# Attention, routing and experts on one core: values in 32-column tiles, sums beside the next pair's values, one-hot matrices in blocks of eight columns

## The chip, the core and the metric

The kernel runs on one core of a Trainium2 chip as one launch. The metric is the device time in microseconds (us). Five engines work side by side and wait for each other through semaphores: PE (TensorE: matmuls; its weight loads are listed apart as PEld), DVE (VectorE), ACT (ScalarE), POOL (GpSimd) and SP, which here only issues transfers.

## The reference, cut to what matters

```python
# 1. attention over 4 batches x 12 heads, 448 rows, head size 64
q_n, k_n = rmsnorm(q, g_q), rmsnorm(k, g_k)
scores = q_n @ k_n.T / 8
attn = softmax(scores)                 # row sums divide the product below
x = (attn @ v)                         # -> [1792 tokens, 768]
# 2. routing: 8 experts, each takes at most 224 of the 1792 tokens
logits = x @ w_gate                    # [1792, 8]
order = argsort(-logits.flatten())     # greedy: best (token, expert) first
# a token goes to the first expert in that order that still has room
# 3. each expert: relu(x[mask] @ w1[e]) @ w2[e]
# 4. h = x @ w_in;  out = (h * cos(h)) @ w_out
```

## The kernel before, in words

The program is written down by a small planner (class `Plan`): every instruction becomes a step with a cost from a table (`Plan.cost`), the data it reads and writes, and a latest time; `Plan.run` then fixes one order for each engine. The order on the chip is that list, and the chip's waits come from the data. The planner knows that PE pays for a change of tile shape (`P.switch`, 0.09 in the attention stage) and prefers the shape it is in (`SAME`).

**Attention** works through 24 pairs of heads. Keys stand on partitions in four chunks of 112. For a pair, `scores` writes exp(scores) of chunk c and head h to a tile `pf` (112 keys x 448 queries); GpSimd adds two chunks to a tile `pa` (ring of `NPA` = 6) for the row sums. `weigh` (L585) then multiplies values by these: for each chunk and head one fp32 matmul with a stationary 112x64 block of `vr` and the 448 columns of `pf` moving, into the 64 partitions of the head in the accumulator `po`. So the array is used as two tiles of 64 columns, one for each head. Two chunks form one `block`, which the planner keeps together; a pair has two of them. ScalarE copies `po` to `xe`. Then come `sums` (L603; row sums with a stationary of ones) and `logits` (L614; gate products of `xe`), fp32 matmuls with 112 moving columns in four tiles of 32 columns, into `dn`. The other matmuls of the stage are `st` (scores) and `s` (a bound of the row maximum; DVE reduces it to `cm`), whose stationary has 64 partitions, so that two of them use the halves of the array by rows, and transposes `t` and the histogram `dn<-ab`, which use the whole array; the transpose of `cm` has 7 columns. `finish(P_ - 1)` (L726) divides by the sums, adds up logits, and transposes `xe` for the token rows. While this goes on, DVE and ACT split weights of the later stages into two fp32r parts (`na`, `nr`) wherever there is room.

**Routing** finds for each expert in turn (t = 0 to 7) the tokens it takes. For t = 0 and 1 it is `quick` (L1005): a threshold is found in three digits of the logits. `count` (L952) builds for each of 16 columns of tokens two one-hot or step matrices `A` and `B` (`AB`; 112x128 bf16, one instruction each, on DVE, ten of the `B` on ACT), and PE multiplies them to a histogram; `digits` (L972) reads off the digit; `narrow` (L985) narrows the search. For t = 0 the first histogram has been built during attention (`start`, L993, one batch at a time), so two counts are left, and for t = 1 three. Then `phase` (L1074) ranks the tokens, builds 16 one-hot matrices `oh` (112x112), and PE turns them into the row numbers `idx`. GpSimd gathers those token rows (`xr<-x,idx`), PE transposes them (`tr`), and expert t starts. For t from 2 on the threshold is found by `slow`, beside the matmuls of earlier experts; only the `oh` part is the same.

**Experts and output.** PE works through two experts, then the cosine part for their 448 tokens, four times. `WARM_B` = 24 matmuls on `oh` keep PE at work while the first gather is under way. `RUSH`, `EARLIER` and `P.rush` are the planner's numbers for how early a routing shall come.

## Time and profile before

| what | us |
|---|---|
| median of 3 runs | 1138.01 (1130.66 to 1146.6) |
| the profiled execution, its own time | 1132.48 |
| its span, first to last instruction | 1130.7 |
| PE busy | 1080.5 (96%) |
| DVE busy | 888.5 (79%) |
| ACT busy | 638.2 (56%) |
| POOL busy | 251.8 (22%) |
| TensorE clock, mean granted share | 0.978 |

An fp32 matmul shows in the trace as two records, so a count of records of `po` or `dn` is twice that of the program's matmuls. A record's end is modelled and overlaps the next one's start; what a run of matmuls costs is read from the start of its first record to the start of the next run. Attention lasts to about 327 us, the first routing to about 364 us, and after that PE works on experts and output to the end.

### The profile page before, as it was taken

Reading aid. Unit: us, or ns where it says so; the run is one execution under the profiler, and the core shown is the slowest. Engines: PE = TensorE matmul, PEld = TensorE weight load, DVE = VectorE, ACT = ScalarE, POOL = GpSimd, SP = SyncE. Lnnn points to the kernel's source line nnn. Section 1 sums busy time; section 2 is a strip of 40 time slices with the busy share of each in tenths; the row PEclk is TensorE's granted clock in tenths of the full one; section 3 lists DMA queues with packets and bytes.
Section 4 is the critical chain, followed back from the end, with each engine's and each line's share of the span. In section 5 each row is a group of like instructions: output and inputs, shape, how many; then the busy total and the mean of one; then the engine's idle time right before and its main releaser. Section 6 shows DMA issues by size and latency. Waiting matters only on the chain.

```text
span 1130.7 us, 20923 instructions
## 1 busy us (share of the span) xinstructions
PE 1080.5 (96%) x7268; PEld 877.6 (78%) x7268; DVE 888.5 (79%) x2453; ACT 638.2 (56%) x1562; POOL 251.8 (22%) x367
## 2 busy tenths in 40 slices
PE   7999999999976999999999999999999999999997
PEld 5555555555535998997989998899989789999887
DVE  8888989999989968998988886568889577756300
ACT  5687878865663437664656672236666236646300
POOL 3677787766510000000110000020000002000001
PEclk9899999999985999999999999999999999999999
DMA  6353455455553798779877668748866958666652
GB/s 163 92 163 110 145 186 170 163 163 177 211 213 97 215 252 297 255 229 383 276 221 205 227 218 251 271 132 238 233 206 218 333 200 243 188 223 208 239 186 94
DMA packets 172745, 234.35 MB, mean 207 GB/s; under 512 B 14112, under 2 KB 144608, under 8 KB 168032
## 3 DMA queue, kind: packets, MB, share of 16 engines
q1 hardware_dynamic: 170240, 222.01, 61.8%
q0 software_dynamic: 2400, 11.01, 2.8%
q8 instruction: 57, 0.93, 0.3%
q14 instruction: 48, 0.39, 0.1%
HBM read 196.37 MB, written 36.52 MB: 206 GB/s over the span
## 4 chain that ended last, share of the span: by engine, by line
PE 41%; issue 14%; DVE 9%; DMA 6%; ACT 1%; POOL 1%; POOLq 0%; SPq 0%; DVEq 0%; ACTq 0%
PE acc L47 39%; DMA xr<-x,idx 2%; DMA ws<-in_moe_w_out_dram 2%; DMA ws<-in_moe_w_dram 2%; DVE oh L47 1%; DVE na L47 1%; DVE wx L47 1%; DVE AB L47 1%; PE rt L47 1%; DVE r L47 1%; PE tr L47 1%; DMA wx<-w_out 0%; ACT wx L1279 0%; POOL xr L1230 0%; DVE gl L47 0%
## 5 line engine op out<-in xcount | busy, mean ns | idle before, releaser
L47 PE MATMUL acc<-wx,gh 128*128 128x512 f32 (+1 forms) x896 | 226.7, 340 | 0.0
L47 PE MATMUL acc<-x2h,wx 128*128 128x448 f32 x768 | 223.0, 368 | 0.0
L47 PEld LDWEIGHTS acc<-wx,gh 128*128 128x128 f32 x896 | 155.7, 190 | 20.7 <-issue 3.0
L47 PEld LDWEIGHTS acc<-x2h,wx 128*128 128x128 f32 x768 | 144.5, 188 | 11.2
L47 PE MATMUL acc<-wx,gl 128*128 128x512 f32 (+1 forms) x448 | 150.6, 336 | 0.0
L47 PE MATMUL acc<-x2l,wx 128*128 128x448 f32 x384 | 140.2, 365 | 0.0
L47 PE MATMUL acc<-gh,wx 128*128 128x448 f32 (+1 forms) x768 | 129.7, 325 | 2.9 <-DVE gh L47 2.7
L47 POOL TENSOR_TENSOR pa<-pf,pf 112x448 f32<-112x448 f32 x94 | 111.8, 1209 | 71.3 <-ACT pf L47 71.2
L47 DVE TENSOR_TENSOR wx<-ws,wx 128x1024 fp32r<-128x1024 f32 (+1 forms) x96 | 104.5, 1089 | 27.2 <-ACT wx L1279 26.4
L47 PEld LDWEIGHTS acc<-gh,wx 128*128 128x128 f32 x768 | 116.4, 191 | 10.8 <-DVE gh L47 2.6
L1230 POOL DMA_INDIRECT xr<-x,idx x16 | 19.4, 1211 | 445.2 <-issue 141.3
L47 ACT ACTIVATE pf<-st 112x448 f32<-112x448 f32 x192 | 93.9, 540 | 42.5 <-PE st L47 40.9
L47 DVE TENSOR_REDUCE cm<-s 128x1 f32<-128x448 f32 x168 | 100.3, 619 | 17.6 <-PE s L47 15.6
L1279 ACT ACTIVATE wx<-ws 128x1024 fp32r<-128x1024 f32 (+1 forms) x96 | 90.7, 947 | 32.1 <-DMA ws<-in_moe_w_dram 16.5
L47 ACT ACTIVATE r<-r 128x448 f32<-128x448 f32 x128 | 74.0, 578 | 53.8 <-DVE r L47 52.0
L47 DVE SCALAR_TENSOR_TENSOR r<-r,acc 128x448 f32<-128x448 int32 (+1 forms) x128 | 77.8, 618 | 32.9 <-ACT r L47 31.4
L47 PE MATMUL acc<-xe,wx 128*128 128x448 f32 x576 | 91.9, 320 | 0.0
L47 PEld LDWEIGHTS acc<-wx,gl 128*128 128x128 f32 x448 | 85.1, 190 | 8.3
L47 PEld LDWEIGHTS acc<-xe,wx 128*128 128x128 f32 x576 | 86.2, 189 | 4.0
L47 PE MATMUL st<-qq,kk 64*112 64x448 f32 x576 | 88.5, 392 | 0.6 <-ACT pf L47 0.5
L47 ACT ACTIVATE oh<-oh 128x896 bf16<-128x896 bf16 x48 | 45.6, 949 | 75.2 <-DVE oh L47 74.9
L1432 POOL DMA_INDIRECT out_dram<-xo,to x14 | 15.6, 1113 | 319.3 <-ACT xo L1400 318.8
(269 smaller groups left out, 1990.3 us busy)
## 6 DMA issues: line engine op xcount, KB each, us to landing
wx<-w_in SPq DMA_DIRECT2D x64, 768.0 KB
wx<-w_out SPq DMA_DIRECT2D x36, 1024.0 KB
ws<-in_moe_w_dram SPq DMA_DIRECT2D x64, 384.0 KB
ws<-in_moe_w_dram SPq DMA_DIRECT2D x48, 512.0 KB
nr<-in_moe_w_in_dram SPq DMA_DIRECT2D x32, 384.0 KB
w_in<-nr SPq DMA_DIRECT2D x32, 384.0 KB
ws<-in_moe_w_out_dram SPq DMA_DIRECT2D x14, 512.0 KB
w_out<-wx SPq DMA_DIRECT2D x14, 512.0 KB
```

The lines of the kernel that those rows point to most:

```text
L47: self.plan.add([(self.eng, self.plan.cost(self.eng, name, out, r, kw), lambda: f(*args, **kw), self.plan.shares(self.eng, name, out, r, k ...
L1230: P.add([("POOL", 2.1 - 0.9 * h, lambda x=x, h=h: nc.gpsimd.indirect_dma_start(out=x, out_offset=None, in_=x_rows, in_offset=bass.Indirect ...
L1279: P.add([("ACT", 0.093 + n * 0.1067, lambda: nc.scalar.activation(hi, s, AF.Copy)), ("DVE", 0.07 + n * 0.0667, lambda: nc.vector.tensor_co ...
L1432: step = nc.gpsimd.indirect_dma_start(out=out, in_=src, in_offset=None, out_offset=bass.IndirectOffsetOnAxis(ap=at, axis=0)).ins
```

## The change

Values: the four 32-column blocks of the two heads' values each get a column tile of their own, so a block has 8 matmuls (two chunks, four tiles) where it had 4. The sums and gate products of pair P - 1 (`count`) are written inside the first values block of pair P, and `finish` follows one pair later; pairs 22 and 23, and the last sums, are taken up separately at the end. `NPA` goes from 6 to 8. In routing, `match` builds eight columns of `A`, `B` or `oh` with one bf16 `tensor_tensor` each, comparing a row of numbers with the columns' values, which are kept twice, side by side; ACT builds none of them any more, except in `start`, which keeps the old form as `signs`. `B` now holds 0 and 1 where it held -1/2 and 1/2, so `digits` halves the total and adds the rank itself. The planner's numbers move too: the price of the new matmuls, `P.switch` 0.09 to 0.18, `WARM_B` 24 to 28, `RUSH` for t = 3.

```diff
--- before.py
+++ after.py
             if name == "matmul" and rhs.dtype == F32 and self.beside:
-                if out.partition_size() == 32:
-                    return 0.05
-                passes *= {32: 0.32, 64: 0.893}.get(out.partition_size(), 1)
+                return 0.05 if out.free_size() <= CP else 0.61
...
-NPA = 6
+NPA = 8
...
         def weigh(P_):
 
-            po, pd = bo()[:, :S], bd()[:, 0:CP]
+            po = bo()[:, :S]
             t = vals.pop(P_).rearrange("p h (c d) -> p h c d", d=D)
             P.beside = True
             for c0 in range(0, NC, 2):
                 def both():
                     for c in range(c0, c0 + 2):
-                        for h in range(2):
-                            pe.matmul(po[h * D:(h + 1) * D], t[:, h, c], exps[P_, h, c], start=c == 0,
+                        for o in range(0, 2 * D, 32):
+                            h, d = divmod(o, D)
+                            pe.matmul(po[o:o + 32], t[:, h, c, d:d + 32], exps[P_, h, c], start=c == 0,
                                       stop=c == NC - 1)
+                    if c0 == 0 and P_ - 1 in open_:
+                        count(P_ - 1)
                 block(both)
-            sums_of[P_] = pd
+                if c0 == 0 and P_ == NPR - 2:
+                    P.beside = False
+                    finish(P_ - 1)
+                    P.beside = True
             outs[P_] = xes()
             sc.activation(outs[P_], po, AF.Copy)
-
-            def sums():
-                for h in range(2):
-                    halves = [c for c in (0, 2) if (P_, h, -1 - c) in exps]
-                    for c in range(0, NC, 2) if len(halves) == 2 else (0, 2, 3):
-                        n, e = CP + (c == 0), exps.pop((P_, h, -1 - c if c in halves else c))
-                        for j in range(NC):
-                            pe.matmul(pd[32 * j:32 * j + 32], ones[0:n, h], e[0:n, j * CP:(j + 1) * CP],
-                                      start=h == 0 and c == 0, stop=False)
-
-            block(sums)
-
-            def logits():
-                for j in range(NC):
-                    pe.matmul(pd[32 * j:32 * j + 32], wg[:, P_ % NP], outs[P_][:, j * CP:(j + 1) * CP], start=False,
-                              stop=True)
-
-            block(logits)
+            open_.add(P_)
+            if P_ >= NPR - 2:
+                block(lambda: count(P_))
             P.beside = False
+        open_ = set()
+        def count(P_):
+            open_.discard(P_)
+            pd = sums_of[P_] = bd()[:, 0:CP]
+            for h in range(2):
+                halves = [c for c in (0, 2) if (P_, h, -1 - c) in exps]
+                for c in range(0, NC, 2) if len(halves) == 2 else (0, 2, 3):
+                    n, e = CP + (c == 0), exps.pop((P_, h, -1 - c if c in halves else c))
+                    for j in range(NC):
+                        pe.matmul(pd[32 * j:32 * j + 32], ones[0:n, h], e[0:n, j * CP:(j + 1) * CP],
+                                  start=h == 0 and c == 0, stop=False)
+            for j in range(NC):
+                pe.matmul(pd[32 * j:32 * j + 32], wg[:, P_ % NP], outs[P_][:, j * CP:(j + 1) * CP], start=False,
+                          stop=True)
...
-            finish(P_ - 1)
+            finish(P_ - 2 + (P_ == NPR - 1))
...
-        P.switch = 0.09
+        P.switch = 0.18
...
+    def twice(self, x):
+        return x.unsqueeze(2).to_broadcast([*x.shape, 2])
+    def match(self, out, row, cols, op):
+        c, n = out.shape[1:]
+        sh = [out.shape[0], c, n // 2, 2]
+        self.nc.vector.tensor_tensor(out.rearrange("p c (n k) -> p c n k", k=2),
+                                     row.rearrange("p (n k) -> p n k", k=2).unsqueeze(1).to_broadcast(sh),
+                                     cols.unsqueeze(2).to_broadcast(sh), op=op)
...
+    def count(self, p, X, W, ab, n, whole=False):
+        nc, P = self.nc, self.P
+        for a in range(0, NCOL, 8):
+            cs = slice(a, a + 8)
+            self.match(ab[:, 0, cs], P["ia"][0:CP], X[:, cs], ALU.is_equal)
+            self.match(ab[:, 1, cs, 0:n], P["ib"][0:CP, 128 - n:], W[:, cs], ALU.is_le)
+            if whole:
+                nc.begin()
+            for c in range(a, a + 8):
+                nc.tensor.matmul(p[:, 0:n], ab[:, 0, c], ab[:, 1, c, 0:n], start=(c == 0), stop=(c == NCOL - 1))
+            if whole:
+                nc.finish()
+    def digits(self, p, n, T, signs=False):
         nc, P, v = self.nc, self.P, self.nc.vector
-        v.tensor_copy(P["tot"], p[:, 0:1].to_broadcast([128, 2]))
+        rp = P["rp2" if signs else "rpt"]
+        if signs:
+            v.tensor_copy(P["tot"], p[:, 0:1].to_broadcast([128, 2]))
+        else:
+            v.tensor_scalar(P["tot"], p[:, 0:1].to_broadcast([128, 2]), 0.5, None, op0=ALU.mult)
+            v.tensor_tensor(rp, P["tot"][:, 0:1].bitcast(F32), P["rp"], op=ALU.add)
         pa = self.psum()
         nc.tensor.matmul(pa[:, 0:2], P["up"], P["tot"], start=True, stop=True)
-        v.scalar_tensor_tensor(P["cmp"][:, 0:n], p[:, 0:n], pa[:, 0:1], P["rp2"].to_broadcast([128, n]), op0=ALU.add,
+        v.scalar_tensor_tensor(P["cmp"][:, 0:n], p[:, 0:n], pa[:, 0:1], rp.to_broadcast([128, n]), op0=ALU.add,
                                op1=ALU.is_ge, accum_out=P["acc"])
...
-        v.scalar_tensor_tensor(P["X"], F, T, X, op0=ALU.subtract, op1=ALU.add)
-        v.scalar_tensor_tensor(P["W"], F, T, W, op0=ALU.is_equal, op1=ALU.mult)
-        v.tensor_tensor(P["X"], P["X"], P["Z"], op=ALU.min)
+        v.scalar_tensor_tensor(P["XF"], F, T, X, op0=ALU.subtract, op1=ALU.add)
+        v.tensor_tensor(P["X"], self.twice(P["XF"]), self.twice(P["Z"]), op=ALU.min)
+        v.scalar_tensor_tensor(P["W"], self.twice(F), T, self.twice(W), op0=ALU.is_equal, op1=ALU.mult)
...
-        v.scalar_tensor_tensor(rel, half, float(-CP), rel, op0=ALU.mult, op1=ALU.add)
+        v.scalar_tensor_tensor(P["rel2"], self.twice(half), float(-CP), self.twice(rel), op0=ALU.mult, op1=ALU.add)
         v.tensor_tensor(pv[:, :, 1], P["pc"], half.unsqueeze(2).to_broadcast([CP, NCOL, 3]), op=ALU.mult)
...
-        for c in range(NCOL):
-            nc.either("tensor_scalar", oh[:, c], P["io"], rel[:, c:c + 1], None, op0=ALU.is_equal)
+        for a in range(0, NCOL, 8):
+            self.match(oh[:, a:a + 8], P["io"], P["rel2"][:, a:a + 8], ALU.is_equal)
         if not first:
...
-RUSH = (15.0, 4.0, 5.0)
+RUSH = (15.0, 4.0, 5.0, 12.0, 5.0, 5.0, 5.0, 5.0)
-WARM_B = 24
+WARM_B = 28
```

**PE, attention, about the tenth pair.** `po` values, `dn<-pa` row sums, `dn<-xe` gate products, `st` scores, `s` bounds; a buffer's number follows the name. Before:

```order
L47 MATMUL st_231<-sr_158,heads 112x448
L47 MATMUL s_229<-kk_147,qq_152 128x448
L47 MATMUL dn_233<-pa_210,ones 32x112 x4
L47 MATMUL dn_233<-pa_206,ones 32x112 x4
L47 MATMUL dn_233<-pa_211,ones 32x112 x4
L47 MATMUL dn_233<-pa_207,ones 32x112 x4
L47 MATMUL dn_233<-xe_216,wg 32x112 x4
L47 MATMUL s_229<-kk_148,qq_153 128x448
```

Now:

```order
L47 MATMUL s_232<-kk_150,qq_155 128x448
L47 MATMUL po_236<-pf_206,vr_170 32x448 x2
L47 MATMUL po_236<-pf_207,vr_170 32x448 x2
L47 MATMUL po_236<-pf_190,vr_170 32x448 x2
L47 MATMUL po_236<-pf_191,vr_170 32x448 x2
L47 MATMUL dn_237<-pa_208,ones 32x112 x4
L47 MATMUL dn_237<-pa_210,ones 32x112 x4
L47 MATMUL dn_237<-pa_209,ones 32x112 x4
L47 MATMUL dn_237<-pa_211,ones 32x112 x4
L47 MATMUL dn_237<-xe_220,wg 32x112 x4
L47 MATMUL st_234<-qq_153,kk_148 112x448
```

Sums and gate products stood between matmuls of other shapes; now they follow values of the same shape, and the values' matmuls are twice as many and half as wide.

**DVE, routing for t = 0, the first count.** `T` is the digit found last, `W` and `X` the columns' values, `ib` and `ia` the rows they are compared with. Before:

```order
L47 SCALAR_TENSOR_TENSOR W<-F_113,T_135,W_120 112x16
L47 SCALAR_TENSOR_TENSOR X<-F_113,T_135,X_117 112x16
L47 TENSOR_SCALAR AB<-ib,W 112x128
L47 TENSOR_TENSOR X<-X,Z 112x16
L47 TENSOR_SCALAR AB<-ib,W 112x128
L47 TENSOR_SCALAR AB<-ia,X 112x128 x6
```

Now:

```order
L47 SCALAR_TENSOR_TENSOR XF<-F_113,T_137,X_117 112x16
L47 SCALAR_TENSOR_TENSOR W<-F_113,T_137,W_120 112x32
L47 TENSOR_TENSOR X<-XF,Z 112x32
L47 TENSOR_TENSOR AB<-ib,W 112x1024
L47 TENSOR_TENSOR AB<-ia,X 112x1024 x2
L47 TENSOR_TENSOR AB<-ib,W 112x1024
```

The shown start of 22 short instructions becomes four long ones; PE's first product of the count needs the first two of them.

**PE, start of the first expert.** `tr` and `acc<-ident,xr` transposes of the gathered rows, `rt<-AB` products of the count for t = 1, `acc<-xo,ws` the expert's matmuls. Before:

```order
L47 MATMUL rt_4230<-tot,up 128x2
L47 MATMUL tr_4228<-ident,xr_4243 128x112 x2
L47 MATMUL tr_4229<-ident,xr_4243 128x112 x2
L47 MATMUL acc_4225<-ident,xr_4243 128x112 x2
L47 LDWEIGHTS ones
L47 MATMUL rt_4231<-acc_133,ones 128x8
L47 MATMUL tr_4228<-ident,xr_4244 128x112 x2
L47 MATMUL tr_4229<-ident,xr_4244 128x112 x2
L47 MATMUL acc_4225<-ident,xr_4244 128x112 x2
L47 MATMUL acc_4226<-xo,ws_4232 128x224 x6
L47 MATMUL acc_4227<-xo,ws_4233 128x224 x2
L47 LDWEIGHTS AB
```

Now:

```order
L47 MATMUL tr_4426<-ident,xr_4441 128x112 x2
L47 MATMUL tr_4427<-ident,xr_4441 128x112 x2
L47 MATMUL acc_4423<-ident,xr_4441 128x112 x2
L47 LDWEIGHTS AB
L47 MATMUL rt_4428<-AB 128x128
...
L47 MATMUL tr_4426<-ident,xr_4442 128x112 x2
L47 MATMUL tr_4427<-ident,xr_4442 128x112 x2
L47 MATMUL acc_4423<-ident,xr_4442 128x112 x2
...
L47 MATMUL acc_4424<-xo,ws_4430 128x224
L47 MATMUL rt_4429<-tot,up 128x2
```

The sixteen products of the second count for t = 1 came behind the expert's first eight matmuls; now eight of them stand between the transposes of the two halves of rows and eight ahead of the expert's first matmul.

## Rows read from the trace of the kernel before

**Rows 1.** The page's head.

```profile
span 1130.7 us, 20923 instructions
```

**Rows 2.** Stretches: length, busy us (instructions) by engine, granted clock, DMA share, GB/s.

```profile
85.00:250.00 165.00, 164.07 (x1538) 95.96 (x1536) 153.19 (x377) 128.35 (x427) 123.36 (x166) 1.00 0.48 154
250.00:330.00 80.00, 73.29 (x680) 41.09 (x676) 74.57 (x183) 50.02 (x114) 41.11 (x39) 0.98 0.56 196
330.00:365.00 35.00, 20.11 (x115) 15.15 (x116) 32.02 (x212) 12.04 (x39) 2.51 (x4) 0.55 0.44 139
365.00:400.00 35.00, 32.59 (x211) 30.12 (x211) 32.74 (x136) 17.61 (x43) 2.72 (x2) 0.97 0.74 220
400.00:1130.70 730.70, 714.58 (x4151) 648.71 (x4149) 525.65 (x1354) 371.66 (x718) 31.66 (x40) 1.00 0.72 231
```

**Rows 3.** PE's timeline, two places in attention: start, length, what, records.

```profile
185.22 1.73 PE L47 MATMUL po<-pf,vr 112*64 112x448 f32 x8
186.88 0.85 PE L47 MATMUL st<-qq,kk 64*112 64x448 f32 x6
187.56 0.36 PE L47 MATMUL st<-sr,heads 64*112 64x448 f32 x2
187.76 0.36 PE L47 MATMUL s<-kk,qq 64*128 64x448 f32 x2
188.06 0.60 PE L47 MATMUL t<-ident,qn 112*128 112x112 f32 x4
...
192.66 0.98 PE L47 MATMUL dn<-pa,ones 113*32 113x112 f32 x32
193.46 0.38 PE L47 MATMUL dn<-xe,wg 128*32 128x112 f32 x8
193.77 0.86 PE L47 MATMUL st<-qq,kk 64*112 64x448 f32 x6
```

**Rows 4.** PEld's timeline: weight loads inside the same values block.

```profile
185.65 0.14 PEld L47 LDWEIGHTS po<-pf,vr 112*64 112x64 f32 x2 [0.23 <-issue]
186.03 0.14 PEld L47 LDWEIGHTS po<-pf,vr 112*64 112x64 f32 x2 [0.23 <-issue]
```

**Rows 5.** Timelines of ACT and PE at the last pair.

```profile
326.28 0.53 ACT L47 ACTIVATE xe<-po 128x448 f32<-128x448 f32 x1
...
326.86 0.40 PE L47 MATMUL dn<-xe,wg 128*32 128x112 f32 x8 [0.57 <-ACT xe L47]
```

**Rows 6.** The chain that ended last, first routing: start, us, what, how many.

```profile
357.17 3.63 DVE AB L47 x22
```

**Rows 7.** DVE's timeline, end of the routing for t = 0.

```profile
348.96 0.42 DVE L47 TENSOR_TENSOR S<-rt,C 112x256 f32<-112x256 f32 x1
...
349.42 0.29 DVE L47 TENSOR_TENSOR A<-S,lim 112x128 f32<-112x128 f32 x1
...
352.04 0.21 DVE L47 TENSOR_TENSOR pv<-pc,half 112x48 bf16<-112x48 bf16 x1
352.16 0.25 DVE L47 TENSOR_SCALAR oh<-io,rel 112x112 bf16<-112x112 bf16 x1
352.33 0.21 DVE L47 TENSOR_TENSOR pv<-pc,pv 112x48 bf16<-112x48 bf16 x1
352.43 2.47 DVE L47 TENSOR_SCALAR oh<-io,rel 112x112 bf16<-112x112 bf16 x15
354.80 0.28 DVE L47 TENSOR_REDUCE m<-La 112x16 f32<-112x128 f32 x1
```

**Rows 8.** PE's timeline ahead of the first expert.

```profile
359.56 1.55 PE L47 MATMUL rt<-AB 112*128 112x128 bf16 x16
362.60 0.27 PE L47 MATMUL rt<-tot,up 128*128 128x2 f32 x1 [1.49 <-DVE tot L47]
...
364.64 1.86 PE L47 MATMUL acc<-xo,ws 128*128 128x224 f32 x4
```

**Rows 9.** PE's waits after 330 us: total, times, longest.

```profile
PE tr L47 <- DMA xr<-x,idx: 5.2, 4, 2.2
```

More of the change, by code (lines that the diff above doesn't have):

```diff
@@ L97, in cost @@
             x.space == bass.MemoryType.PSUM for x in r)
+        fast = fast or (name == "tensor_tensor" and n > 64 and all(x.dtype == BF16 for x in [out] + r))
         return 0.068 + n / (1920.0 if fast else 960.0) + small * (0.061 if name == "scalar_tensor_tensor" else 0.03)
@@ L853, in __init__ @@
         self.first_free()
-        for name in ("m", "mx", "K", "F0", "F1", "Z", "X0", "X1", "X2", "W0", "W1", "W2", "G", "Q", "X", "W", "g"):
+        for name in ("m", "mx", "K", "F0", "F1", "Z", "X0", "X1", "X2", "W0", "W1", "W2", "G", "Q", "XF", "g"):
             t(name, [CP, NCOL])
+        for name in ("X", "W"):
+            t(name, [CP, NCOL, 2], BF16)
         for name in ("t0", "t1"):
@@ L861, in __init__ @@
         t("acc", [128, 1])
+        t("rpt", [128, 1])
         t("acc8", [128, E], BF16)
@@ L907, in on @@
         t("rel", [CP, NCOL])
+        t("rel2", [CP, NCOL, 2], BF16)
     def flip(self, out, k, tmp):
@@ L950, in parts, with signs @@
             v.tensor_scalar(c[n], i, add, WIDE, op0=ALU.add, op1=ALU.mult)
-    def count(self, p, X, W, ab, n, whole=False):
+    def twice(self, x):
[6 more added lines that the diff above has]
+                                     cols.unsqueeze(2).to_broadcast(sh), op=op)
+    def signs(self, p, X, W, ab):
         nc, P = self.nc, self.P
@@ L956, in count @@
         for c in range(cols):
-            A, B, ib = ab[:, 0, c], ab[:, 1, c, 0:n], P["ib"][0:CP, 128 - n:]
+            A, B, ib = ab[:, 0, c], ab[:, 1, c], P["ib"][0:CP]
             if c * SIGNS % 16 < SIGNS:
@@ L963, in count @@
                 nc.either("tensor_scalar", A, P["ia"][0:CP], X[:, c:c + 1], 2.0, op0=ALU.is_equal, op1=ALU.mult)
-            if not whole:
-                nc.tensor.matmul(p[:, 0:n], A, B, start=(c == 0), stop=(c == cols - 1))
-        if whole:
-            nc.begin()
-            for c in range(cols):
-                nc.tensor.matmul(p[:, 0:n], ab[:, 0, c], ab[:, 1, c, 0:n], start=(c == 0), stop=(c == cols - 1))
-            nc.finish()
-    def digits(self, p, n, T):
-        nc, P, v = self.nc, self.P, self.nc.vector
-        v.tensor_copy(P["tot"], p[:, 0:1].to_broadcast([128, 2]))
+            nc.tensor.matmul(p, A, B, start=(c == 0), stop=(c == cols - 1))
+    def count(self, p, X, W, ab, n, whole=False):
[11 more added lines that the diff above has]
+    def digits(self, p, n, T, signs=False):
+        nc, P, v = self.nc, self.P, self.nc.vector
+        rp = P["rp2" if signs else "rpt"]
[4 more added lines that the diff above has]
+            v.tensor_tensor(rp, P["tot"][:, 0:1].bitcast(F32), P["rp"], op=ALU.add)
         pa = self.psum()
         nc.tensor.matmul(pa[:, 0:2], P["up"], P["tot"], start=True, stop=True)
-        v.scalar_tensor_tensor(P["cmp"][:, 0:n], p[:, 0:n], pa[:, 0:1], P["rp2"].to_broadcast([128, n]), op0=ALU.add,
+        v.scalar_tensor_tensor(P["cmp"][:, 0:n], p[:, 0:n], pa[:, 0:1], rp.to_broadcast([128, n]), op0=ALU.add,
                                op1=ALU.is_ge, accum_out=P["acc"])
@@ L998, in start @@
         p = self.psum()
-        self.count(p, P["X0"][:, s], P["W0"][:, s], ab, 128)
+        self.signs(p[:, 0:128], P["X0"][:, s], P["W0"][:, s], ab)
         if q == 0:
@@ L1012, in quick @@
             p = ps()
-            self.count(p, P["X0"], P["W0"], P["AB"], 128, True)
-        self.digits(p, 128, T[0])
+            v.tensor_copy(P["X"], self.twice(P["X0"]))
+            v.tensor_copy(P["W"], self.twice(P["W0"]))
+            self.count(p, P["X"], P["W"], P["AB"], 128, True)
+        self.digits(p, 128, T[0], first)
         self.narrow(P["F0"], T[0], P["X1"], P["W1"])
@@ L1143, in close @@
         v.tensor_scalar(P["rp"], P["rp"], 1.0, None, op0=ALU.max)
-        v.tensor_scalar(P["rp2"], P["rp"], 2.0, None, op0=ALU.mult)
         self.first_free()
@@ L1172 @@
 REST = 64
-EARLIER = 140
+EARLIER = (140, 140, 140, 140)
 MAGS = 4
@@ L1443, in fetch @@
             if t < E:
-                P.rush = RUSH[min(t, 2)]
+                P.rush = RUSH[t]
                 route(t, step)
@@ L1459, in moe @@
                 expert(t, j)
-            behind = chain[-EARLIER]
+            behind = chain[-EARLIER[GROUPS.index(grp)]]
             P.rush = 100.0
```

## The prediction

> **What bounds the kernel now.** I read the page's head first, then a table of stretches, then the timelines of PE and DVE in the stretches that the change touches, and PE's waits last. The profiled span is 1130.7 us [rows 1]. The stretches show three regimes [rows 2]. From 85 to 250 us, in the middle of attention, PE is busy 164.07 of 165 us and DVE 153.19: PE's list of instructions sets the pace, and what it loses it loses inside that list. From 250 to 330 us PE falls to 73.29 of 80 while DVE has 74.57: there DVE leads by a little. From 330 to 365 us, the first routing, PE is busy 20.11 of 35 us at a clock of 0.55, DVE 32.02: one chain through DVE with short visits to PE. After 400 us PE is busy 714.58 of 730.7, and only single waits are left.
>
> The reader is to see in PE's timeline what a change of tile shape costs [rows 3, 4]. A values block runs from 185.22 to 186.88, 1.66 us. Its pairs of weight loads lie 0.38 apart (185.65, 186.03), and that is one step, two tiles of 64 columns at work together with 448 columns each. Four steps are 1.5; 0.15 is left over. In `dn`, 32 records in four tiles of 32 columns take 192.66 to 193.46, 0.80 for eight steps; the last two steps, 0.20, last 0.31 until the scores begin, so 0.11 goes with leaving the shape. A bound `s`, one step of 0.20 (187.56 to 187.76 is such a step), takes 0.30 up to the transposes: 0.10 for leaving again. Three steps of scores from 186.88 to 187.56 take 0.68, 0.08 over. So a change costs about 0.10 for leaving and 0.10 for entering the 64-row shape; entering column tiles costs what is left of the block's 0.15, 0.05; for entering the whole array I take nothing (0.10 at most, as for the others).
>
> **The change part by part.**
>
> *Values.* The work per step stays: 448 columns, four steps a block, 48 blocks, 192 steps. No row shows four tiles with 448 columns. The nearest is `dn`, four tiles with 112 columns: 0.80 less 0.05 for entering, over eight steps, is 0.094, times four 0.375. The ends are 0.375 (all four together) and 0.75 (only two at a time). I take 0.375, since `dn` is the same shape and type, and its four tiles read four different pieces: nothing gained, nothing lost.
>
> *Changes of shape.* This is where the gain is. With sums and gate products behind values of the same shape, the drain between them goes. Counted along PE's two orders, attention has 291 changes before and 242 now. Class by class, at the prices above, they cost 45.9 and 37.8 us: 8.1 less. By place it is 2.3 in the first eight blocks (to 85 us), 3.8 from there to the 38th (259 us), and 2.0 in the last ten. In the middle PE is full, and I count all 3.8. At the start PE has filler matmuls and waits, so half, 1.2. At the end DVE leads [rows 2], and I count none. Together -5.0; the ends are -1 and -8.
>
> *Sums one pair later.* `finish`, with its DVE and ACT work and the store of token rows on SP, moves back by about half a pair to a pair; nobody needs its rows before the stage ends, and the longer life of `pa` is covered by `NPA` = 8. Three `finish` crowd the end instead. There the last sums now stand in one block with the gate products and wait for ScalarE's `xe` (326.28, 0.53 long; gate products at 326.86 [rows 5]), while before they ran ahead of it. If ScalarE comes as late as before, this costs the length of the sums, 1.4; if it comes right after the values, nothing. I take +0.3.
>
> *First routing.* Before, a count is 22 short instructions in 3.63 us [rows 6], 0.165 each, and 16 `oh` take 352.16 to 354.80, 2.64 [rows 7]. Now a count is four long instructions of 1024 elements (the second count has two of 512), `oh` two of 896. What one costs no row shows. Two fp32 operands go at 0.13 us for 128 elements (0.42 against 0.29), so 1024 elements cost at most 1.1; the lower end is the 0.16 of one short instruction. The nearest row for two bf16 operands is `pv<-pc,pv`: its successor starts 0.10 later (352.33, 352.43), while `pv<-pc,half` with an fp32 operand needs 0.12 (352.04, 352.16). The 0.02 saved are half of what 48 elements cost at the fp32 rate. So I take half that rate: 0.6, 0.34 for 512, 0.54 for `oh`. [...] Against that, PE could follow column by column; now eight products wait for the last instruction, at 0.10 each (16 in 1.55 [rows 8]), 0.8. First count 2.4 + 0.8 against 3.7: -0.5. Second 1.9 + 0.8 against 3.4: -0.7. `oh` 1.1 + 0.8 against 2.7: -0.8. The row numbers for t = 0 come 2.0 earlier.
>
> *Start of the first expert.* That does not bring it 2.0 earlier. PE already waited 1.49 there for the routing of t = 1, not for rows [rows 8], and now all sixteen products of that routing's second count stand ahead of the expert's first matmul. The chain is 2.0 ahead and its first count 1.2 shorter, but the second count (2.4 + 0.8) lies on it: 364.64 - 3.2 + 3.2, no change (between -2 and +1). The sixteen products no longer stand in the expert's own stretch: -1.0. Four more filler matmuls lie in the same wait: nothing.
>
> *Later routings.* The routing for t = 1 ends some 2 us earlier and `oh` is 1.4 shorter each time; DVE isn't the bound there (525.65 of 730.7). PE's four waits for gathered rows are 5.2, the longest 2.2 [rows 9]. In PE's new order the longest, for t = 6, has 51 expert matmul rows between `oh` and its transposes, before 36; at some 0.2 each that covers it: -2.0. The one for t = 1: -1.0. The others stay.
>
> Sum: -5.0 + 0.3 - 1.0 - 2.0 - 1.0 = -8.7, from the profiled execution's own 1132.48 to 1123.8. The median of the three runs, 1138.01, lies 5.5 above that execution, and the four together average 1136.9. I put the new median 3 above the sum: **1127**.
>
> **The rivals.**
>
> *DVE takes over in attention.* For: 153.19 of 165 us already, and the weight splitting cannot shrink. Against: the gaps left there are 12 us, three times the 3.8 asked for. Then attention gives 1.5 in place of 4.7: 1130.
>
> *Long instructions at the fp32 rate.* Then each of 1024 elements costs 0.5 more. On the path lie four and three in the counts for t = 0, two of `oh`, eight in the counts for t = 1: 2.0 + 1.5 + 0.9 + 4.0 = 8.4 back, 1135. Against: the 0.02 of `pv`.
>
> *Four tiles don't keep step (slower).* The place is the 192 steps of the values; the price is what a step takes above 0.375. From 0.42 on (8.7 / 192 = 0.045) the whole gain is gone, and the kernel is slower; with two tiles at a time it is 72 us, 1199. For: each tile now reads 448 columns, and both tiles of a head read the same ones. Against: the `dn` steps. [...]
>
> *More than the drains goes.* Between 250 and 330 us PE idles 6.7 us behind DVE. If the later `finish` and the longer `pa` ring take half of that away, and the last 2.0 count as well: 1121.
>
> **How the numbers follow.** Forecast 1127, 0.45; DVE bound 1130, 0.2; fp32 rate 1135, 0.1; four tiles, 0.08; more, 1121, 0.12; something else in the new order, 0.05. The range takes in the first three, the larger gain, the ends of the attention term, and the 8 us by which runs of one program lie on either side of their median: 1114 to 1142. What a measurement can tell here is 2%, 23 us. Faster by that needs three times the sum, 0.05. Slower by that needs a step above 0.55, half of the third rival's cases: 0.04. The rest is within 2%: 0.91.
>
> **What would show it.** Right: values blocks of 16 records still 1.5 us long plus 0.05, with `dn` following without a gap; DVE's `AB<-ib,W` at 0.6 from start to start; first expert matmul as far behind the end of attention as now; no wait for rows at t = 6. Wrong: a step above 0.4; a long `AB` at 1.1; DVE without gaps from 100 us on, and PE with them; a clock that stays at half past the first expert's start.

## The result, and the profile after

The change is slower: 1153.86 us median of 6 runs (1151.73 to 1155.27) beside 1134.99 for the kernel before (6 runs), a ratio of 1.0147 with a 95% interval of 1.0113 to 1.0182 (estimated over the runs; the quotient of the two medians is 1.0166). The forecast was 1127, with a range up to 1142. It stayed within the 2% to which the prediction gave 0.91, but on the other side of before. The profiled execution took 1154.0 us. Its head, where [rows 1] had 1130.7:

```profile
span 1152.2 us, 21451 instructions
```

The stretches of the kernel after (columns as in [rows 2]; a row is shifted against before by what has been lost up to there), and last all of attention from 30 us to the start of the last histogram product `dn<-ab`, at 345.36:

```profile
85.00:250.00 165.00, 155.02 (x1656) 91.27 (x1648) 157.48 (x364) 123.05 (x416) 121.32 (x159) 0.99 0.53 166
250.00:330.00 80.00, 72.69 (x730) 40.77 (x732) 71.01 (x171) 46.01 (x101) 38.22 (x41) 0.96 0.51 171
365.00:400.00 35.00, 31.46 (x213) 29.93 (x214) 32.26 (x135) 5.11 (x12) 3.05 (x4) 0.79 0.64 188
400.00:1152.20 752.20, 731.25 (x4222) 661.31 (x4221) 524.98 (x1273) 379.26 (x730) 30.47 (x42) 0.99 0.73 229
...
30.00:345.36 315.36, 291.87 (x3022) 169.33 (x3019) 281.41 (x674) 218.13 (x699) 202.91 (x263) 0.97 0.48 152
```

The same last stretch of the kernel before, where that product started at 331.26:

```profile
30.00:331.26 301.26, 289.38 (x2631) 167.34 (x2630) 275.03 (x678) 220.95 (x707) 202.63 (x264) 0.98 0.49 160
```

The loss is here. Attention is 14.1 us longer. PE, full from 85 to 250 us before (164.07 of 165), is busy 155.02 now. Over the whole stretch it idles 315.36 - 291.87 = 23.5 us, before 11.9. Its busy time is 2.5 longer although work went away: summed over pieces of 3 us, (1 - granted clock) x busy time, an estimate of what the half clock (a granted share of 0.50) cost, is 9.6 us, before 5.0. So 11.6 us more idle, 4.5 more lost to the half clock, and 2.0 less work make up the 14.1.

The work holds filler matmuls from the start of the stage, `po<-ab`, which compute nothing that is used. The new order leaves more of them behind 30 us; PE's groups in the last stretch above, first before, then after:

```profile
L447 PE MATMUL po<-ab 112*128 112x256 bf16 x32 | 5.0, 286 | 0.0
```

```profile
L446 PE MATMUL po<-ab 112*128 112x256 bf16 x48 | 9.6, 317 | 0.0
```

If each record counts from its start to the next one's, without waits and times the granted clock, the fillers are 5.9 us of work, before 3.9, and the rest of PE's work is 276.0 us, before 280.2 (the six runs of the order of before, listed below, show 280.2 to 282.5). So the change did save some 4 us of PE's work in attention, and its order lost more than four times that. Behind attention another 7 us are lost, from the last histogram product to the last matmul 800.3 us against 793.1.

The block that was to get shorter did. PE's timeline (start, length, what, records), to compare with [rows 3]:

```profile
190.83 1.71 PE L47 MATMUL po<-pf,vr 112*32 112x448 f32 x16
192.35 0.96 PE L47 MATMUL dn<-pa,ones 113*32 113x112 f32 x32
193.13 0.38 PE L47 MATMUL dn<-xe,wg 128*32 128x112 f32 x8
193.44 0.88 PE L47 MATMUL st<-qq,kk 64*112 64x448 f32 x6
```

Values take 1.52 from start to the sums, sums and gate products 1.09. In the kernel before nine of the values blocks stand ahead of sums too: there two tiles of 64 columns take 1.654 in the median, and sums and gate products behind them 1.105. The pair of blocks is 0.15 shorter. Before another shape four tiles still take 1.64.

What PE waits for in this stretch now, 85 to 250 us (total, times, longest):

```profile
PE s L47 <- DVE cm L47: 7.5, 10, 1.8
PE dn L47 <- DVE ab L47: 1.9, 1, 1.9
```

In the kernel before the same view has one line:

```profile
PE s L47 <- DVE cm L47: 0.9, 3, 0.4
```

The bound products `s` have two buffers in the kernel, which DVE's reductions `cm` read: the ten waits of 7.5 us in all are PE's `s` waiting for a `cm`. DVE's groups in the same stretch say who waits for whom (busy, mean ns, then DVE's idle time before them and its cause), first before:

```profile
L47 DVE TENSOR_REDUCE cm<-s 128x1 f32<-128x448 f32 x97 | 58.2, 619 | 9.1 <-PE s L47 7.7
...
L47 DVE TENSOR_SCALAR na<-na 128x384 f32<-128x384 f32 (+1 forms) x39 | 16.2, 436 | 0.1
L47 DVE TENSOR_TENSOR nr<-na,nr 128x384 fp32r<-128x384 f32 x20 | 12.6, 638 | 0.0
```

and after:

```profile
L47 DVE TENSOR_REDUCE cm<-s 128x1 f32<-128x448 f32 x92 | 54.6, 614 | 2.2 <-PE s L47 1.8
...
L47 DVE TENSOR_SCALAR na<-na 128x384 f32<-128x384 f32 (+1 forms) x39 | 19.6, 529 | 0.2 <-ACT na L47 0.2
L47 DVE TENSOR_TENSOR nr<-na,nr 128x384 fp32r<-128x384 f32 x20 | 14.4, 726 | 2.6 <-ACT nr L47 2.2 <-DMA sr<-cr 0.2
```

Before, DVE came early and waited 7.7 us for PE. Now it waits 1.8, and PE waits 7.5 for it. That is an exchange of places: a quarter of the waiting on one side, eight times as much on the other. DVE's weight splitting has become dearer too (436 to 529 ns, 638 to 726), of which more below; whether that made the exchange, no run shows.

The wait of 1.85 us cost more than itself. PE's timeline around it, and the stretches there:

```profile
209.72 0.72 PE L47 MATMUL dn<-ab 112*128 112x128 bf16 x3 [1.85 <-DVE ab L47]
...
211.68 3.02 PE L47 MATMUL po<-pf,vr 112*32 112x448 f32 x16
214.52 0.95 PE L47 MATMUL dn<-pa,ones 113*32 113x112 f32 x32
```

```profile
205.00:210.00 5.00, 2.92 (x19) 1.85 (x18) 5.00 (x12) 3.48 (x14) 4.50 (x5) 1.00 0.26 84
210.00:215.00 5.00, 4.90 (x46) 2.05 (x49) 4.86 (x16) 2.76 (x10) 0.00 (x0) 0.66 0.21 82
215.00:220.00 5.00, 5.00 (x70) 2.23 (x66) 4.67 (x18) 4.27 (x25) 3.60 (x2) 1.00 0.35 94
```

PE is busy 2.92 of 5 us, and behind that the granted clock is 0.66 on average, 0.50 from 211 to 214 us. The values block there takes 2.84 in place of 1.53; another, from 288.70 on and with the clock at 0.50 all through, takes 2.98.

First routing, DVE's timeline; the answer to [rows 6, 7]:

```profile
349.19 0.69 DVE L47 TENSOR_TENSOR AB<-ib,W 112x1024 bf16<-112x1024 bf16 x1 [0.24 <-DVE X L47]
349.80 1.29 DVE L47 TENSOR_TENSOR AB<-ia,X 112x1024 bf16<-112x1024 bf16 x2
351.00 0.69 DVE L47 TENSOR_TENSOR AB<-ib,W 112x1024 bf16<-112x1024 bf16 x1
...
364.69 1.16 DVE L47 TENSOR_TENSOR oh<-io,rel 112x896 bf16<-112x896 bf16 x2
365.77 0.21 DVE L47 TENSOR_TENSOR pv<-pc,pv 112x48 bf16<-112x48 bf16 x1
```

A long instruction takes 0.60 from start to start (349.19, 349.80, two to 351.00), and `oh` 0.54, as forecast. Behind the first routing, at t = 1, PE waits 2.08 us for `pv`, where it waited 0.8 before:

```profile
398.42 1.38 PE L47 MATMUL rt<-pv,oh 112*112 112x6 bf16 x16 [2.08 <-DVE pv L47]
```

```profile
398.00:402.00 4.00, 3.58 (x22) 3.40 (x22) 2.38 (x11) 2.06 (x4) 0.00 (x0) 0.58 0.83 237
402.00:406.00 4.00, 4.00 (x14) 3.64 (x14) 3.18 (x9) 2.05 (x3) 2.56 (x2) 0.56 0.52 140
```

Again a wait of 2 us, and the clock near half for most of 8 us behind it.

### The profile page after: what moved, and what is told of

Read it like the earlier page. It is cut to its first block, busy times and chain, and to the rows that moved or that the text cites. A ratio compares the mean times of both kernels' runs of the same rounds, so it can differ in the third digit from the quotient of the medians.

```text
span 1152.2 us, 21451 instructions
## 1 busy us (share of the span) xinstructions
PE 1084.2 (94%) x7656; PEld 880.7 (76%) x7656; DVE 879.7 (76%) x2250; ACT 623.8 (54%) x1512; POOL 250.3 (22%) x369
## 4 chain that ended last, share of the span: by engine, by line
PE 55%; DVE 25%; DMA 9%; ACT 6%; issue 3%; SPq 1%; POOL 0%; POOLq 0%; DVEq 0%; ACTq 0%
PE acc L47 43%; DVE na L47 5%; DMA ws<-in_moe_w_dram 5%; DVE cm L47 4%; PE st L47 3%; PE po L47 3%; ACT sq L47 2%; DVE wx L47 2%; DVE r L47 2%; DMA wx<-w_out 1%; PE s L47 1%; ACT pf L47 1%; PE rt L47 1%; DVE oh L47 1%; DVE nr L47 1%
## 5 line engine op out<-in xcount | busy, mean ns | idle before, releaser
L47 POOL TENSOR_TENSOR pa<-pf,pf 112x448 f32<-112x448 f32 x94 | 114.3, 1235 | 81.0 <-ACT pf L47 71.5
L47 PE MATMUL st<-qq,kk 64*112 64x448 f32 x576 | 93.1, 397 | 1.0 <-ACT pf L47 0.9
L47 PE MATMUL po<-pf,vr 112*32 112x448 f32 x768 | 85.2, 560 | 0.0
```

Of the source, the lines that this page charges most:

```text
L47: self.plan.add([(self.eng, self.plan.cost(self.eng, name, out, r, kw), lambda: f(*args, **kw), self.plan.shares(self.eng, name, out, r, k ...
```

## The experiments

The first theory was that the planner's new order loses what the shape gains; the runs were to find which part of the change makes it bad. "Start" is that of the last histogram product, "idle" PE's idle time from 30 us to there, "half clock" the time lost to it, as defined above; the ratio is to the kernel before, with its interval.

| run | order of attention | start | idle | half clock | ratio |
|---|---|---|---|---|---|
| before | its own | 331.3 | 11.9 | 5.0 | |
| e1 tiles kept | as before | 328.0 | 11.8 | 0.0 | 0.9977 (0.9948 to 1.0005) |
| e3 routing alone | as before | 329.3 | 11.0 | 1.7 | 1.0006 (0.9977 to 1.0036) |
| e7 routing, pad | as before | 333.4 | 10.8 | 3.3 | 1.0009 (0.9982 to 1.0036) |
| g3 second plan | as before | 328.8 | 12.4 | 0.0 | 1.0019 (0.9991 to 1.0046) |
| g4 old numbers | as before | 327.7 | 10.9 | 1.7 | 1.0038 (1.0016 to 1.0059) |
| the change | new | 345.4 | 23.5 | 9.6 | 1.0147 (1.0113 to 1.0182) |
| e2 its price at 0.09 | new | 339.7 | 15.5 | 8.0 | 1.0086 (1.0063 to 1.0110) |
| g2 its price at 0.10 | new | 340.6 | 21.3 | 6.5 | 1.0134 (1.0086 to 1.0181) |
| e5 cheap values | new | 342.8 | 20.1 | 9.9 | 1.0163 (1.0108 to 1.0218) |
| e6 cheap values, 0.09 | new | 342.9 | 25.8 | 3.4 | 1.0154 (1.0112 to 1.0196) |
| f3 own class, 0.09 | new | 341.8 | 20.0 | 7.7 | 1.0120 (1.0076 to 1.0163) |
| e4 before, price 0.18 | new | 346.3 | 16.7 | 6.6 | 1.0113 (1.0061 to 1.0165) |
| f1 before, price 0.10 | new | 347.1 | 21.0 | 9.3 | 1.0139 (1.0096 to 1.0181) |
| g1 before, price 0.08 | new | 329.1 | 13.2 | 1.7 | 1.0071 (1.0039 to 1.0104) |
| e8 tiles, planned freely | new | 351.9 | 25.3 | 7.8 | 1.0189 (1.0146 to 1.0231) |
| f2 tiles, own class | new | 339.6 | 18.6 | 6.0 | 1.0042 (1.0015 to 1.0068) |
| f4 as e8, no bonus | new | 345.0 | 21.4 | 6.5 | 1.0088 (1.0058 to 1.0118) |

**The shape alone.** The values in four tiles, every instruction of the other engines and of PE in its old place (the planner is told the old cost and the old class):

```diff
-for h in range(2):
-    pe.matmul(po[h * D:(h + 1) * D], t[:, h, c], exps[P_, h, c], ...)
+for h, d in ((0, 0), (0, 32), (1, 0), (1, 32)):
+    pe.matmul(po[h * D + d:h * D + d + 32], t[:, h, c, d:d + 32], exps[P_, h, c], ...)
```

> The kernel before with nothing but the shape of the values changed: four tiles of 32 columns in place of two of 64, every instruction of every engine in the order of before, routing as before. Theory 1 (the shape is good, the new order loses): blocks of values that are followed by sums fall from 1.65 to 1.53 us, the others stay within 0.05; attention, whose last histogram product started at 331.3 us before, ends 0 to 4 us earlier there (327 to 331); total 0 to 5 us less than before. Rival (four tiles cost something that the blocks alone do not show, such as clock or late weight loads): attention ends at 335 or later, as part of the 345.4 of the change.

It took 1132.37 us beside 1134.62. Its stretches:

```profile
85.00:250.00 165.00, 163.96 (x1802) 95.53 (x1796) 153.61 (x379) 129.19 (x429) 122.41 (x167) 1.00 0.49 156
...
30.00:328.01 298.01, 286.23 (x3028) 163.70 (x3027) 276.04 (x683) 222.79 (x719) 207.66 (x265) 1.00 0.51 164
```

PE is as full as before, and everything came as theory 1 had it. Of the 3.3 us by which attention ends earlier, 2.3 were there at the first values block, ahead of which the kernel before has a wait of 2.16 us and half a clock (0.50 from 40 to 45 us) and this run has neither (1.00 there). That is scatter: attention of before itself ends between 327.7 (g4) and 333.4 (e7). The lengths of the blocks say what the shape gives: 8 blocks ahead of sums are 0.126 shorter, 38 others 0.013, and the sums behind those 8 are 0.051 longer, 1.1 us in all. It costs nothing: the rival that four tiles don't keep step is out. This is the one kernel of the set whose median is below that of before, by an interval that still holds "the same".

**The price of a change of shape.** One number, in the change and in the kernel before:

```diff
-P.switch = 0.18
+P.switch = 0.09    # e2, in the change; e4: 0.09 to 0.18 in the kernel before
```

> The change with the planner's price of a change of shape put back from 0.18 to 0.09 us; all else is as changed. Theory 1a (the price of 0.18 makes the planner group shapes, so bound products and their reductions come in bursts and PE waits for DVE): PE's waits for reductions between 85 and 250 us fall from 7.5 to below 3, the last histogram product starts at 335 or earlier, against 345.4; total 8 to 14 us below the change. Rival 1b (sums inside the next pair's values block and the later finish make the waits): at most 4 us come back, the product starts at 341 or later.

> The kernel before, with the planner's price of a change of shape at 0.18 in place of 0.09 us and nothing else. Theory 1a: the price alone spoils the order; PE's waits for reductions rise above 5 us between 85 and 250 us and the last histogram product starts at 339 or later, against 331.3. Rival 1b: it stays between 328 and 334.

e2 gets 5.6 of the 14.1 us back, 8.5 us in the median (1145.32), and still starts that product 8.5 later than before; the waits for reductions from 85 to 250 us fell to 1.1 us. So theory 1a had the waits and the total right and the start wrong, and 1b, which gave back at most 4 us, is out. e4 loses 15.0 with nothing changed but the price. Its start is in 1a's bounds, its waits for reductions are not (3.8 from 85 to 250 us), and its loss is made otherwise than the change's: 4.8 more idle, 1.6 more lost to the half clock, and 8.6 more work, of which 4.2 are fillers behind 30 us. The price matters, but it is not the whole, and bursts of reductions are not what it acts by alone.

**Is it the planner's idea of PE's speed?** Values planned at 1.06 us a block in place of 1.55:

```diff
-return 0.05 if out.free_size() <= CP else 0.61
+return 0.05 if out.free_size() <= CP else 0.3625    # e5; e6 with P.switch = 0.09 too
```

> The change with one planner cost altered: the first matmul of each group of four values tiles is planned at 0.3625 us in place of 0.61, so that a values block is planned at 1.06 us while it takes 1.53 to 1.64. The price of a change of shape stays at 0.18, and the instructions are the same. Theory 2 (what counts is whether the planner's PE is slower or faster than the chip's: planned too slow, DVE's list holds other work ahead of the reductions and PE waits for them; planned a little too fast, DVE waits for PE, which costs nothing): DVE's idle time before reductions rises from 3.7 to over 8 us, PE's waits for reductions between 85 and 250 us fall from 7.5 to below 3, the last histogram product starts at 337 or earlier, against 345.4. Rival (the price of 0.18 hurts because like shapes are grouped, whatever PE's speed in the plan): it stays at 342 or later.

> As the run before, and the price of a change of shape at 0.09 too. Theory 2: PE is planned faster still; the last histogram product starts at 334 or earlier (339.7 with the price alone), and PE's idle time and half-clock time in attention together come down to about that of the kernel before (17 us). Rival (any new order of this planner scatters by several us, whatever its costs): between 336 and 346, with no order among the three kernels that follows the planned speed.

Both failed theory 2: 342.8 and 342.9. PE's waits for reductions between 85 and 250 us did come down, to 3.2 and 3.9, and DVE's idle time before them from 45 to 340 us went up, to 11.0 and 12.0 from 4.8 in the change, but the time didn't follow: other waits took their place. That there is no order by planned speed, the rival in the second, fits.

**Is it the moved sums, or the class?** e8 plans the four tiles freely in the structure of before (sums in blocks of their own); f2 is e8 with values as a class of their own; f3 is the change with that class and the old price; f4 is e8 without the bonus for staying in a shape:

```diff
-for h in range(2):
-    pe.matmul(po[h * D:(h + 1) * D], t[:, h, c], ...)
+for o in range(0, 2 * D, 32):                            # e8, with the cost of the change
+    h, d = divmod(o, D)
+    pe.matmul(po[o:o + 32], t[:, h, c, d:d + 32], ...)
+s.mode = (..., 64 if w.name.startswith("vr") else ...)   # f2 beside e8; f3 in the change
+SAME = 0.0                                               # f4 beside e8, was 8.0
```

> The kernel before with values in four tiles of 32 columns, planned as the change plans them (cost 0.61 and the shape of the sums, price of a change 0.09), but sums and gate products as blocks of their own behind their pair, and the finish where it was; routing as before. Theory 1b (sums in the next pair's block and the later finish make the waits): the last histogram product starts at 333 or earlier. Theory 3 (the planner's freedom to mix values and sums is enough to give the worse order): at 336 or later, as with the change at the same price (339.7).

> The kernel before with values in four tiles of 32 columns at the change's planned cost (1.55 us a block, before 1.56), but counted by the planner as a shape of their own, as before, and not as that of the sums. That is the only difference from the run with the tiles planned freely (351.9). Theory 4: the last histogram product starts at 327 to 334, total 1128 to 1138. Theory S: the 0.01 us in the cost redraw part of the order, and it starts at 336 or later.

> The change with values counted by the planner as a shape of their own and the price at 0.09 (the two that the planner saw in before); sums in the next pair's values block, the later finish, the longer ring and routing as changed. Theory 4: the last histogram product starts at 335 or earlier, against 339.7 with the price alone. Theory S, or the moved sums: at 337 or later.

> As the run with the tiles planned freely (values and sums one shape, price 0.09, structure of before; the last histogram product at 351.9), with the planner's bonus for a step of the same shape at 0 in place of 8 us. Theory 4 by way of the bonus (values and sums of one shape are preferred by 8 us over bound products and transposes, so those come late and in bursts): PE's waits for DVE and its half-clock time in attention fall by half, it starts at 340 or earlier. Theory S: anywhere from 335 to 355, with waits at other places.

e8 is the worst of all (1157.23 us) without any of the moved sums, so they are not needed for the loss. Its stretch and PE's longest waits, 30 us to the end of attention:

```profile
30.00:351.90 321.90, 296.64 (x3028) 166.18 (x3026) 289.88 (x681) 224.09 (x719) 206.44 (x265) 0.97 0.47 152
```

```profile
PE t L47 <- DVE part L47: 7.2, 4, 3.6
PE s L47 <- DVE cm L47: 5.9, 9, 1.3
PE dn L47 <- DVE ab L47: 3.2, 3, 1.8
```

The weights are others than in the change, where `cm` leads with 11.4: here transposes that wait for `part` come first. f2 gets over half of e8's loss back but is 8 us late at 339.6, though the planner saw only 0.01 us of cost that differs from before; f3 and f4 are late too. Theory 4 explains a part of e8 at most.

**Scatter.** The kernel before, with nothing else changed:

```diff
-P.switch = 0.09
+P.switch = 0.10    # f1; g1: 0.08
```

> The kernel before with the planner's price of a change of shape at 0.10 in place of 0.09 us, nothing else. Theory S (scatter: the order of before is one draw that was chosen among many, and any other draw of this planner is worse by 5 to 20 us, whatever the reason for the new draw): the last histogram product starts at 336 or later, against 331.3 (328.0 to 333.4 in the three runs of that very order). Theory 4 (the draws differ because values and sums now count as one shape; a price of 0.01 more is harmless): 327 to 334.

> The kernel before with the planner's price of a change of shape at 0.08 in place of 0.09 us. Theory S (the order of before is one chosen draw): the last histogram product starts at 336 or later, against 328 to 333 for the order of before; total 5 to 20 us above before. Rival (a lower price is harmless or better, 0.10 was only on the wrong side): 333 or earlier.

f1 has the same 7268 records on PE as before, a part of them in attention at other places of the list, and costs as much as the whole change: 1153.31 us against 1136.23. Its stretch:

```profile
30.00:347.06 317.06, 296.06 (x2638) 170.00 (x2637) 280.66 (x679) 220.93 (x715) 204.24 (x265) 0.97 0.47 153
```

One place makes up over half of it, some 9 of 15.8 us. DVE's timeline, then PE's, and the stretches there:

```profile
56.36 1.48 DVE L47 SCALAR_TENSOR_TENSOR na<-nr,na 128x384 int32<-128x384 int32 x1
57.77 1.28 DVE L47 TENSOR_SCALAR na<-na 128x384 int32<-128x384 int32 x1
58.97 1.48 DVE L47 SCALAR_TENSOR_TENSOR na<-nr,na 128x384 int32<-128x384 int32 x1
60.37 0.67 DVE L47 SCALAR_TENSOR_TENSOR kk<-t,gcol,kk 128x448 fp32r<-128x448 f32 x1
```

```profile
61.19 0.98 PE L47 MATMUL t<-ident,qn 112*128 112x112 f32 x4 [5.00 <-DVE kk L47]
62.10 3.25 PE L47 MATMUL po<-pf,vr 112*64 112x448 f32 x8
```

```profile
55.00:60.00 5.00, 1.19 (x11) 0.62 (x8) 5.00 (x5) 1.61 (x3) 5.00 (x6) 1.00 0.93 288
60.00:65.00 5.00, 3.81 (x12) 1.43 (x12) 2.39 (x4) 1.07 (x2) 2.85 (x5) 0.50 0.21 53
```

Weight splitting stands ahead of `kk` in DVE's list, runs at more than twice its usual time (1.48 and 1.28 us; the medians are 0.55 and 0.35) beside a GpSimd that is busy throughout, PE waits 5.0 us, and then works at half clock (0.50 from 60 to 65 us). g1 missed its mark: the product starts at 329.1. It lost some 7 us just behind, where nine splitting instructions stand between the last histogram and the first routing:

```profile
330.93 1.42 DVE L47 SCALAR_TENSOR_TENSOR na<-nr,na 128x512 int32<-128x512 int32 x2
332.26 0.88 DVE L47 TENSOR_SCALAR na<-na 128x512 f32<-128x512 f32 x2
...
336.74 0.16 DVE L47 CAST tot<-hist 128x2 fp32r<-128x2 f32 x1
```

PE's next product waits 7.0 us for that (0.7 before). Nearly 9 us more were lost later, in the second plan's order of before. The total is 1144.00 us against 1136.60, inside what theory S gave for it; the rival's "harmless" is out, though its mark for the start is met. With the change:

> The change with the price at 0.10 (345.4 for the start of the last histogram product at 0.18, 339.7 at 0.09). Theory S: another draw, anywhere from 335 to 350, its PE waits at other places than at 0.09. Rival (the price acts smoothly): within 1.5 us of 339.7.

It took 1150.72 us and starts at 340.6. That lies in both theories' bounds, and doesn't tell them apart; its longest waits ahead of the last histogram product do begin at other places than that of e2 (2.62 at 45.7, 2.19 at 214.1, against 2.01 at 289.8).

**Routing.** Attention in the order of before, routing as changed:

```diff
+P.pad = 1.0 * (t > 0)                      # e7, was (t > 1); e3 without it
+RUSH = (15.0, 4.0, 5.0, 5.0, ...); WARM_B = 24    # g4: the old numbers
```

> Attention as before, in the order of before; routing, its turns and the fillers as changed. Theory 1: attention ends as before (331.3), the one-hot matrices of the first routing come 0.6 us earlier after it than before (20.7 in place of 21.3), and the 7.4 us that the change loses behind attention come back here in full: total 5 to 9 us above before. Rival (what is lost behind attention comes from the shifted start of the weights' transfers, not from routing): total within 2 us of before, or below it.

> Attention as before, routing as changed (as in the run of routing alone, 1136.8 us), and in the plan every routing step of PE for t = 1 is due 1.0 us after its inputs, as those for t = 2 and later already are. Theory (the shorter chain is planned to reach PE sooner than DVE can deliver; PE then waits 2.1 us for the products of t = 1 and its clock stays at half behind that wait for some 7 us): the wait falls below 0.8 us, the clock stays full between 380 and 392 us, total 3 to 6 us below the run of routing alone. Rival (the wait only moves to the gathered rows of t = 1): total within 1.5 us of that run.

> Attention as before, routing as changed, but with the old numbers: turn 3 hurried by 5 in place of 12 us, 24 fillers in place of 28. From the last histogram product to the last matmul routing as changed took 800.2 us. If the new numbers cost the time: 794 to 796. If the long instructions and the order that they bring cost it: 799 or more.

and of the kernel before, with one number of the second plan:

```diff
-RUSH = (15.0, 4.0, 5.0)
+RUSH = (15.0, 4.0, 5.2)
```

> The kernel before with the hurry of the routings from t = 2 on at 5.2 in place of 5.0 us; attention keeps its order, 55 of PE's 5768 rows stand otherwise behind it. From the last histogram product to the last matmul before took 793.1 us. Theory S for the second plan too: 796 or more. Rival (the second plan is not so touchy; long instructions or the new numbers cost the 6 to 7 us): 792 to 795.

From that product to the last matmul: e3 800.2 us, e7 797.0, g4 801.3, and before's routing 793.1 (before), 794.2 (e1). But runs whose second plan is that of before, behind other orders of attention, show 796.0 (f1), 797.3 (f4), 798.2 (e8), 799.7 (e4), 801.8 (f2) and 808.6 (g1, its wait of 7.0 included), and g3 799.2 with 55 of PE's rows moved, though g3's median is that of before (1137.70 beside 1136.60). So one profile of this stage scatters by up to 9 us with no change to it, g1 left aside, and the 7 us that the change lost there can't be laid on routing by one profile. The medians say that routing alone is worth about nothing: 1136.79 us beside 1134.62 (e3), 1137.07 beside 1135.82 (e7); the 5 to 9 us that e3's theory laid on it are not there. With the old numbers it is 0.4% slower (g4, 1140.27 beside 1136.60), so these don't cost the time. In e7 the wait of 2.1 us at t = 1 and the half clock behind it (0.50 from 384 to 388 us in e3, 1.00 from 370 to 386 in e7) went as expected, but smaller waits came from 386 to 394 us with the clock at 0.81 there, and no gain can be told in the total.

## Why the prediction was wrong

*The step that failed* is the premise "PE is full", on which the middle's drains were counted as time saved. PE was full in the order of before. The change gives the planner another class, another price and other blocks, so it writes another order for five engines, and whether PE is full in that one stood in no row. I priced "something else in the new order" at 0.05 and gave it no time. It was 16.1 us in attention: 11.6 idle and 4.5 lost to the half clock. The drains themselves did go; the new order took their gain, and more, in waits.

- *Values.* Right: four tiles keep step, with 1.52 to 1.64 for the whole block, where two tiles took 1.654.
- *Changes of shape.* -5.0 was forecast. Without the fillers PE's work in attention shrank by 4.2, about as forecast, but it did not become time. The size hangs on the order as well: five other orders of the changed program show 275.6 (e5) to 280.7 us (e2) of such work, the change 276.0. With the order held (e1) only 8 blocks stand ahead of sums, and the shape gave 1.1.
- *Sums one pair later.* +0.3 was forecast; from the start of the last records of values to the last histogram product it is 5.4 us, before 6.8. Both times the product waits for DVE's `ab` (2.82 here), so the sums don't set the end.
- *First routing.* Lengths right. The last product of the row numbers starts 22.0 us behind the last histogram product, before 23.7: 1.7 earlier (2.0 forecast). The first expert's first matmul stands 33.5 us behind the last histogram product, before 33.4: no change, as forecast.
- *Later routings.* The wait at t = 6 is gone, and so is the longer one for rows at t = 1. But 2.08 us for `pv` and the clock of 0.58 and 0.56 behind it, and 2.3 at 908 us for `w_out`, came in their place. -3.0 was forecast here and -1.0 for products moved out of the expert's stretch; none of it shows in the totals of e3 and e7, which have this routing behind the attention of before (1.0006 and 1.0009). These 4 us failed too.
- *Rivals.* "DVE takes over" named the right pair of engines and the wrong price: 1130, because it let PE lose no more than the gain. From 85 to 250 us DVE had waited 7.7 us for PE and been early; in the change it is late, and PE pays the wait and sometimes the clock behind it (1.7 us of work behind the wait of 1.85). But that is this order's way, not that of all slow ones: in f1 and e8 DVE's reductions wait 13.8 and 13.2 us for PE in this stretch, and PE loses its time at other places.

All twelve redrawn orders, six of them of a program that differs from before by no instruction or by the shape of the values alone, are slower than before by their intervals; the five kernels that keep its order in attention lie within 0.4% of it. That the order of before was picked among many is argued, not shown; that its neighbours are worse is shown. What stays open is which property of an order keeps PE full: neither price, planned speed, class nor bonus sorts the twelve. No run has the moved sums and the later `finish` in an order that was held, so whether they cost something of their own in the change is open too; e8 shows that as much is lost without them.

## What to carry to other kernels

Where a list scheduler writes the order and its numbers were tuned, the kernel's time is that of one selected order. Before pricing what an edit saves, ask whether the order survives it: if not, price the redrawing, by moving a number that changes nothing else (here 0.01 us, 17 us of time), or hold the old order for a first measurement of the edit, and search for a new order afterwards (no such search was run here).

## What the runs showed of the hardware that I had not expected

- A wait of PE of 1 to 5 us in attention was in some places followed by several us at half clock: in the change 3.4 us at 0.50, 1.7 us of work lost, behind a wait of 1.85, in f1 a values block of 3.2 us in place of 1.65 behind a wait of 5.0. Not always: of the change's eight waits of 1 us or more from 30 to 340 us, six left the clock at 1.00 for the 4 us behind them, the one of 1.83 us ahead of 122.5 among them, and the clock fell to 0.50 at 36.9 us behind none above 0.9. In the same attention one wait had the half clock behind it in the kernel before (2.16 us, then 0.50) and not in g3 (2.15 us, then 1.00):

```profile
38.92 0.46 PE L47 MATMUL s<-kk,qq 64*128 64x448 f32 x1 [2.16 <-DVE cm L47]
```

```profile
40.00:45.00 5.00, 5.00 (x48) 3.03 (x49) 3.88 (x10) 1.61 (x7) 2.70 (x3) 0.50 0.63 146
```

```profile
40.24 0.46 PE L47 MATMUL s<-kk,qq 64*128 64x448 f32 x1 [2.15 <-DVE cm L47]
```

```profile
40.00:45.00 5.00, 4.76 (x55) 2.72 (x57) 4.81 (x12) 2.25 (x11) 3.86 (x6) 1.00 0.33 89
```

- DVE instructions sometimes take more than twice their usual time, 1.48 in place of 0.55 us in f1. In the change's attention, from 30 us on, 52 of DVE's instructions take over 1.25 times the median of their own kind (operation, tiles and shape) and 0.05 us more; GpSimd works beside each for a part of it, for 36 over nine tenths. Over those medians they cost 33.4 us, before 22.3, in e8 38.5. Yet 242 more have GpSimd beside them for over nine tenths and keep their time, so what decides was not found. Nor does this sum sort the orders: it is 22.0 in e4, which starts the last histogram product at 346.3.
- Four column tiles with 448 columns each run at the pace of two (a block 1.64 us, two tiles 1.654), and a block of four tiles is 0.11 shorter ahead of sums, which have its shape, than ahead of another (1.53 against 1.64).
